# Delta rule in chunks: token products on 32-row tiles of the array, the state summed in PSUM

## The chip, the cores and the metric

The kernel runs on one core of a Trainium2 chip. The metric is the device time of one execution in microseconds (us), and lower is better. Five engines work side by side and meet at semaphores: PE (TensorE: "PE" rows are its matrix products, "PEld" rows the loads of its stationary operand), DVE (VectorE), ACT (ScalarE), POOL (GpSimd) and SP, which here only issues transfers (DMA). Each engine runs its own instructions in the order in which they were written down for it.

## The reference

Two blocks follow each other, all in fp32: a delta rule over 768 tokens (4 batch rows, 8 heads, head size 48), and a mixture of 8 experts with 4 slots each.

```python
k_n = k / (norm(k) + 1e-6)
for t in range(S):                       # S = 768; state: (B, H, 48, 48)
    y[:, :, t] = einsum('bhd,bhde->bhe', q[:, :, t], state)
    v_old = einsum('bhde,bhd->bhe', state, kt)
    state = state + bt * einsum('bhd,bhe->bhde', kt, vt - v_old)
x = y as (B*S, H*D) = (3072, 384)
logits = x @ phi                         # 32 slots
d = softmax of logits over the tokens;   slot_input = d.T @ x
slot_out[e] = relu(slot_input[e] @ w1[e]) @ w2[e]        # 8 experts, F = 1024
c = softmax of logits over the slots;    out = c @ slot_out
```

## The kernel before

The tokens are cut into 24 chunks of 32. Four chunks make a group, and there are six groups. On the 128 partitions lie four heads times 32 tokens (partition 32 h + t); the other head half g and the batch row b are looped over, so eight "units" u = (b, g) make up a chunk. In a chunk, with the state S before it:

    (I + L) w = V - Kn S,  L[t, s] = beta_s kn_t.kn_s (s < t),  u_s = beta_s w_s
    y = Q S + strict_lower(Q Kn^T) u,      S += Kn^T u

Names used below, with the lines of the kernel before. `psR` (L310) is Kn S, `R` (L314) is V minus it on DVE. `psW` (L324) is the inverse T applied to R, `U` (L329) is psW times beta on DVE. `psS` (L340) is Kn^T u, and `S` (L345) the state after it on DVE. `psY` gets Q S (L354) and then the strictly lower product with U (L359), and ACT copies it to `Y` (L362). A product over 32 tokens of each of four heads is made here with one stationary operand of 128x128 that is zero outside its four diagonal blocks: `TT` holds the inverse so, `AT` (L233) the lower product so, spread by DVE with the mask `bdm`, and `KX` (L291) the keys, spread by POOL with the mask `hm`. The chunk is worked in two halves `hf` of two batch rows each, so that DVE can work on one while PE works on the other.

What doesn't depend on the state runs one group ahead. `norm` scales the keys (`sq` L185, `ssq` L186, `Ks` L199). `prep` transposes keys and queries (L215, ACT copies them to `KQ`, L218) and makes the products over the head size (L230; ACT copies one half to `Lc`, L232, DVE makes `AT`). `invert` sends Lc through DRAM to the layout "one 32x32 block per partition" (`ld`, `lb`), multiplies by beta on POOL (L252), eliminates 31 columns on DVE (two instructions each, L264 and L267), and stores the inverse `tt` to DRAM (`td`). `near` loads a chunk's inverse from there into one of two `TT` buffers (L282). `route` makes logits (transposes L379, ACT copy `yT` L381, products with phi L385), both softmaxes, and the slots' weighted sums (`d` spread over heads L443, `db` on POOL L453, products L458) of the group before.

These steps are lists which `fill` interleaves with a chunk's chain: two `prep` in each of the chunks 0 and 1 of a group, `near`, half of `invert` and of `route` in chunk 2, the rest in chunk 3. A scheduler then sets each engine's final order. After the six groups come the routing of the last group, the experts (`ph` L557, `pso` L568) and the output (`pout` L588). Two experts' first weights `w1t` are loaded near the start; the others when the first block's memory is free. A matrix product in fp32 shows as two instructions in the profile, so 192 calls of L324 are 384 rows; transposes show as one.

Of the kernel before, what the change touches and what calls it, by code (L numbers as in the profile page):

```python
# [16 lines left out]
def kernel(  # L17
# [45 lines left out]
    wk = att.enter_context(tc.tile_pool(name="wk", bufs=2))  # L63

# [4 lines left out]
    Ks = [io.tile([P, GC, U, DP], F32, name=f"Ks{i}", bufs=1) for i in range(2)]  # L69
# [11 lines left out]
    def load_k(n, eng=nc.sync):  # L81
        load(k, Ks[n % 2], n, eng)
# [10 lines left out]
    NB = NCH // 3  # L93
    bts = []
    for i, tag in enumerate(("Lc", "lb", "tt")):
        t = wk.tile([U, NB, 4, C], F32, name=f"bt{i}", tag=tag, bufs=2 if tag == "tt" else 1)
        for h in range(4):
            nc.gpsimd.dma_start(
                out=t[:, :, h, :],
                in_=beta.rearrange("b (g h) (c t) -> h (b g) c t", h=4, t=C)[  # L100
                    h, :, i * NB:(i + 1) * NB])
        bts.append(t)
    # the same by blocks: partition 32 h + 8 c + u of a group of chunks
# [11 lines left out]
    for g in range(G):  # L115
# [12 lines left out]
                            pattern=[[C, 4]], channel_multiplier=-1)  # L128
    bdm = cpool.tile([P, 4, C], F32, name="bdm")
# [3 lines left out]
    nc.vector.tensor_tensor(bdm, bdm, hm.unsqueeze(2).broadcast_to([P, 4, C]), op=ALU.mult)  # L133
    sel = cpool.tile([P, GC, 4, C], F32, name="sel")
# [5 lines left out]
    bta = cpool.tile([P, NCH, U], F32, name="bta")  # L140
    pb = pt([P, NCH, U])
    for c in range(NCH):
        nc.tensor.transpose(pb[:, c, :], bts[c // NB][:, c % NB].rearrange("p h t -> p (h t)"),
                            ident[0:U, 0:U])
    nc.vector.tensor_copy(bta, pb)

    TTs = [wk.tile([P, U, 4, C], F32, name=f"TT{i}", bufs=1) for i in range(2)]
    for t in TTs:
        nc.vector.memset(t, 0.0)
    psS = ps.tile([P, 2, 4, D], F32, name="psS")  # L150
    nc.vector.memset(psS, 0.0)
    St = []
    for i in range(2):
        t = wk.tile([P, 2, 4, D], F32, name=f"S{i}", tag=f"S{i}")
        nc.vector.memset(t, 0.0)
        St.append(t)

# [16 lines left out]
    # Each of these gives a list of steps, which the chunks' chain is interleaved with.  # L174
    KQ, AT, KX, Lc, TTb = {}, {}, {}, {}, {}

    def norm(n):
        Kf = Ks[n % 2].rearrange("p c u d -> p (c u) d")
# [4 lines left out]
        def squares():  # L183
            sq = wk.tile([P, GC * U, D], F32, name="sq", tag="KX")
# [19 lines left out]
    def prep(n, c):  # L204
        """Of a chunk: Kn and Q transposed, strict_lower(Q Kn^T) and Kn Kn^T (both transposed)."""
        cc = n * GC + c

        def transposes(bh):
# [3 lines left out]
            for i in range(2):  # L212
                b = 2 * bh + i
                for a, src in enumerate((Ks[n % 2], Qs)):
                    nc.tensor.transpose(  # L215
                        tp[:, i, a, :],
                        src[:, c, b * G:(b + 1) * G, :].rearrange("p g d -> p (g d)"), ident)
            nc.scalar.activation(KQ[cc][:, 2 * bh:2 * bh + 2], tp, ACT.Copy)  # L218

        def products(g):  # L220
            if g == 0:
                AT[cc] = wk.tile([P, G, B, 4, C], F32, name="AT", tag="AT", bufs=2 * GC - 1)
                if c == 0:
                    Lc[n] = wk.tile([P, GC, B, G, C], F32, name="Lc", tag="Lc", bufs=1)
            r = slice(DP * g, DP * g + D)
            pg = pt([P, B, 2, C])
            for b in range(B):
                for h in range(4):
                    rh = slice(C * h, C * h + C)
                    nc.tensor.matmul(pg[rh, b], lhsT=KQ[cc][r, b, 0, rh], rhs=KQ[cc][r, b, :, rh],  # L230
                                     start=True, stop=True, skip_group_check=True)
            nc.scalar.activation(Lc[n][:, c, :, g, :], pg[:, :, 0, :], ACT.Copy)  # L232
            nc.vector.tensor_tensor(  # L233
# [389 lines left out]
```

## Time and profile before

| | |
|---|---|
| median of 3 runs | 919.21 us (918.97 to 921.51) |
| profiled execution, first to last instruction | 919.5 us |
| its mean granted TensorE clock | 0.701 |
| start, up to the first psW product | 97 us |
| group 0, up to the transposes in group 1 | 97 to 190 us |
| groups 1, 2 and 3 | 114.5, 114.8 and 115.4 us |
| group 4, up to the first psW product of group 5 | 127 us |
| group 5 | 48 us |
| routing of group 5, experts, output | 28, 151 and 31 us |

No time of the profiled execution outside its span is given; its span lies 0.3 us above the median, so the two are taken as the same. A timeline row reads: start in us, length in us, engine, line, operation, result and operands, shape, number of instructions, and in brackets how long the engine was idle before and what released it. A row of the stages reads: the stretch, its length, each engine's busy time (and instructions), the granted TensorE clock (1.00 is full speed), the share of DMA and its GB/s. A row of groups by line ends with "busy us, mean ns of one | idle before, releaser".

### The profile page before, as it was taken

The page shows a single profiled execution, that of the slowest core. Times are in us where ns is not written, and L with a number is a line of the kernel's source. Part 1 is how long each engine was busy: PE and PEld are TensorE (multiplying, and loading weights), DVE is VectorE, ACT ScalarE, POOL GpSimd, SP SyncE. Part 2 cuts the span into 40 slices and gives each one's busy share as a digit, 9 for nine tenths or more (in the row PEclk, how much of TensorE's full clock was granted, in tenths as well). Part 3 has the DMA queues.
Part 4 walks back from the last instruction along what each step waited for, and adds up shares of the span by engine and source line. Part 5 has one row for each costly group of instructions (what it writes and reads, how often), then busy time and mean ns, then how long its engine had stood idle before and what let it go on. Part 6 is the DMA issues. An engine that isn't in the chain of part 4 may idle for free.

```text
span 919.5 us, 19108 instructions
## 1 busy us (share of the span) xinstructions
PE 679.9 (74%) x8324; PEld 565.6 (62%) x8324; DVE 299.4 (33%) x816; ACT 101.3 (11%) x223; POOL 192.9 (21%) x347
## 2 busy tenths in 40 slices
PE   1706569069990799807998069996499799999998
PEld 1504569058880688706888058885398696765754
DVE  3267112942139421394213942226421100000011
ACT  0303000021120211102111021111000110000001
POOL 7231213131251213412134111351210200000000
PEclk9999999999995555755557555565555567667765
DMA  6240763023310242102321021000100099990013
GB/s 118 37 85 26 133 115 72 1 52 55 75 20 0 58 70 55 20 0 58 69 55 19 0 58 32 25 2 0 35 13 1 1 266 211 237 231 16 1 60 146
DMA packets 148019, 58.12 MB, mean 63 GB/s; under 512 B 131968, under 2 KB 143328, under 8 KB 147936
## 3 DMA queue, kind: packets, MB, share of 16 engines
q1 hardware_dynamic: 141888, 55.87, 27.9%
q10 hardware_dynamic: 5664, 0.94, 0.6%
q8 instruction: 65, 1.06, 0.5%
q0 software_dynamic: 384, 0.10, 0.1%
q14 instruction: 18, 0.15, 0.1%
HBM read 45.86 MB, written 11.01 MB: 62 GB/s over the span
## 4 chain that ended last, share of the span: by engine, by line
PE 64%; DVE 17%; DMA 6%; POOL 4%; SPq 3%; ACT 3%; issue 2%; ACTq 0%; DVEq 0%; POOLq 0%
PE ph L557 9%; PE psW L324 8%; PE psY L359 7%; DVE pr L264 7%; PE pso L568 6%; PE psS L340 6%; DVE tt L267 6%; PE pt L215 5%; PE pt L385 5%; PE pt L458 3%; PE pout L588 3%; PE psR L310 2%; PE pt L230 2%; PE psY L354 2%; PE pt L379 2%; SPq L77 2%
## 5 line engine op out<-in xcount | busy, mean ns | idle before, releaser
L215 PE MATMUL pt<-ident,Ks 128*128 128x128 f32 x96 | 42.1, 438 | 167.9 <-POOL Ks L199 158.7
L291 POOL TENSOR_TENSOR KX<-Ks,hm 128x192 f32<-128x192 f32 x184 | 91.0, 531 | 354.0 <-PE psS L340 264.4
L215 PEld LDWEIGHTS pt<-ident,Ks 128*128 128x128 f32 x96 | 20.8, 216 | 173.9 <-POOL Ks L199 159.6
L324 PE MATMUL psW<-R,TT 128*128 128x48 f32 x384 | 86.6, 396 | 34.4 <-DMA TT<-td 31.2
L324 PEld LDWEIGHTS psW<-R,TT 128*128 128x128 f32 x384 | 81.1, 311 | 39.4 <-DMA TT<-td 19.1
L557 PEld LDWEIGHTS ph<-sacc,w1t 96*128 96x128 f32 x512 | 87.8, 272 | 3.8 <-issue 3.8
L557 PE MATMUL ph<-sacc,w1t 96*128 96x4 f32 x512 | 88.1, 310 | 0.0
L359 PE MATMUL psY<-U,AT 128*128 128x48 f32 x384 | 83.9, 393 | 0.0
L264 DVE TENSOR_TENSOR pr<-tt,lb 128x31 f32<-128x31 f32 (+15 forms) x186 | 76.7, 413 | 16.2 <-POOL lb L252 11.0
L359 PEld LDWEIGHTS psY<-U,AT 128*128 128x128 f32 x384 | 78.2, 306 | 3.4
L267 DVE TENSOR_TENSOR tt<-tt,pr 128x31 f32<-128x31 f32 (+15 forms) x186 | 73.3, 394 | 5.2
L340 PE MATMUL psS<-U,KX 128*48 128x48 f32 x1472 | 69.8, 271 | 0.0
L340 PEld LDWEIGHTS psS<-U,KX 128*48 128x48 f32 x1472 | 60.8, 181 | 6.3 <-issue 1.7
L568 PE MATMUL pso<-w2t,hx 128*32 128x384 f32 x128 | 58.5, 627 | 1.7 <-DVE hx L561 1.7
L329 DVE TENSOR_TENSOR U<-psW,bta 128x192 f32<-128x192 f32 x48 | 17.2, 358 | 113.4 <-PE psW L324 113.4
L345 DVE TENSOR_TENSOR S<-S,psS 112x384 f32<-112x384 f32 x46 | 25.5, 554 | 87.6 <-PE psS L340 87.3
L233 DVE TENSOR_TENSOR AT<-pt,bdm 128x512 f32<-128x512 f32 x48 | 31.9, 688 | 62.1 <-ACT Lc L232 59.0
L385 PE MATMUL pt<-phi,yT 96*128 96x32 f32 x192 | 45.1, 398 | 6.0 <-ACT yT L381 5.1
L230 PE MATMUL pt<-KQ 48*32 48x64 f32 x1536 | 47.5, 310 | 1.9
L385 PEld LDWEIGHTS pt<-phi,yT 96*128 96x128 f32 x192 | 42.0, 323 | 10.5 <-ACT yT L381 9.1
L561 DVE TENSOR_SCALAR hx<-ph 128x32 f32<-128x32 f32 x8 | 1.5, 192 | 141.0 <-PE ph L557 141.0
L354 PE MATMUL psY<-S,KQ 48*32 48x48 f32 x1536 | 46.1, 265 | 0.1
(107 smaller groups left out, 698.9 us busy)
## 6 DMA issues: line engine op xcount, KB each, us to landing
w1t<-in_moe_w_dram SPq DMA_DIRECT2D x16, 768.0 KB
w2t<-in_moe_w_dram SPq DMA_DIRECT2D x8, 1536.0 KB
Ks<-in_k_dram SPq DMA_DIRECT2D x96, 48.0 KB
V<-in_v_dram SPq DMA_DIRECT2D x96, 48.0 KB
out_dram<-ob SPq DMA_DIRECT2D x24, 192.0 KB
Qs<-in_q_dram SPq DMA_DIRECT2D x80, 48.0 KB
ld<-Lc SPq DMA_DIRECT2D x24, 128.0 KB
lb<-ld SPq DMA_DIRECT2D x6, 512.0 KB
```

Source lines behind the costliest of these rows:

```text
L215: nc.tensor.transpose(tp[:, i, a, :], src[:, c, b * G:(b + 1) * G, :].rearrange("p g d -> p (g d)"), ident)
L230: nc.tensor.matmul(pg[rh, b], lhsT=KQ[cc][r, b, 0, rh], rhs=KQ[cc][r, b, :, rh], start=True, stop=True, skip_group_check=True)
L264: nc.vector.tensor_tensor(prv, tt[:, 0:m, j:j + 1].broadcast_to([P, m, w]), lb[:, j, j + 1:C].unsqueeze(1).broadcast_to([P, m, w]), op=ALU ...
L267: nc.vector.tensor_tensor(tt[:, 0:m, j + 1:C], tt[:, 0:m, j + 1:C], prv, op=ALU.subtract)
L291: nc.gpsimd.tensor_tensor(KX[cc][:, g, b], kn[:, b].unsqueeze(1).broadcast_to([P, 4, D]), hm.unsqueeze(2).broadcast_to([P, 4, D]), op=ALU. ...
L324: nc.tensor.matmul(pw[:, i, g, :], lhsT=T[:, (2 * hf + i) * G + g].rearrange("p h t -> p (h t)"), rhs=Rs[hf][:, i, g, :], start=True, stop ...
L340: nc.tensor.matmul(psS[DP * g:DP * g + D, i, h, :], lhsT=kx[:, g, 2 * hf + i, h, :], rhs=Us[hf][:, i, g, :], start=True, stop=True, skip_g ...
L354: nc.tensor.matmul(py[C * h:C * h + C, b, :], lhsT=kq[r, b, 1, C * h:C * h + C], rhs=old[b // 2][r, b % 2, h, :], start=(b == 0), stop=Fal ...
L359: nc.tensor.matmul(py[:, b, :], lhsT=at[:, g, b].rearrange("p h t -> p (h t)"), rhs=Us[b // 2][:, b % 2, g, :], start=False, stop=True, sk ...
L385: nc.tensor.matmul(pl, lhsT=yT[:, h].rearrange("p c t -> p (c t)"), rhs=phi[:, h, :], start=(h == 0), stop=(h == 3))
L557: nc.tensor.matmul(st["ph"][:, t, :], lhsT=w1t[e][:, h, t * P:(t + 1) * P], rhs=sacc[:, h, sl], start=(h == 0), stop=(h == 3))
L568: nc.tensor.matmul(pso, lhsT=hx[:, e, t, :], rhs=w2t[e][:, t, :], start=(e == 0 and t == 0), stop=(e == E - 1 and t == NFC - 1))
```

## The change

Every product over 32 tokens now uses four tiles of 32 rows of the array, one for each head, instead of one stationary operand of 128x128 with zeros. For psW and the lower part of psY, head h uses rows 32h to 32h+31 and columns 32h to 32h+31, and all four write one PSUM bank on different partitions. For psS, head h uses rows 32h and on, 48 columns at 64 g, and each head writes its own bank. So `TT` and `AT` lose their zeros, `KX` is gone (the keys are read where they lie), and `tri`, the mask of one head, takes the place of `bdm`.

The state is no longer added on DVE: psS stays in four PSUM banks and sums over all chunks, and after each chunk ACT copies the half g = 0 and DVE the half g = 1 into one of two state buffers. That state holds, for each head, the two g blocks on its diagonal, so psR and Q S are each 16 calls with 128 rows and 96 columns moved, where they were 32 calls with 48 rows and 48 columns. The beta of U is multiplied into the inverse before its store, by one POOL instruction. The two halves of a chunk are merged: one R, one U, one Y copy in a chunk. psR and psW share one bank, psY has one bank, and there are three key buffers instead of two. The products of `prep` take g innermost, into two buffers at once. `fill` counts four calls in a chunk instead of five. The beta loads and transposes of the start (`bts`, `bta`) are gone.

```diff
-    TTs = [wk.tile([P, U, 4, C], F32, name=f"TT{i}", bufs=1) for i in range(2)]
-    psS = ps.tile([P, 2, 4, D], F32, name="psS")
+    TTs = [wk.tile([P, U, C], F32, name=f"TT{i}", bufs=1) for i in range(2)]
+    psS = psp.tile([P, 4, 512], F32, name="psS")
...
         def store():
+            nc.gpsimd.tensor_tensor(st["tt"], st["tt"],
+                                    bb[:, n].unsqueeze(1).broadcast_to([P, C, C]), op=ALU.mult)
...
+            pg = [pt([P, B, 2, C]) for _ in range(G)]
             for b in range(B):
                 for h in range(4):
+                    for g in range(G):
...
+            for g in range(G):
+                nc.scalar.activation(Lc[n][:, c, :, g, :], pg[g][:, :, 0, :], ACT.Copy)
+                nc.vector.tensor_tensor(AT[cc][:, g], pg[g][:, :, 1, :],
+                                        tri.unsqueeze(1).broadcast_to([P, B, C]), op=ALU.mult)
...
-        def keys(g):
...
+        for a, dst in enumerate((pr, py)):
+            for b in range(B):
+                for h in range(4):
+                    nc.tensor.matmul(dst[hs[h], b].rearrange("p g d -> p (g d)"),
+                                     lhsT=kq[:, b, a, hs[h]], rhs=old[:, h, b, :],
+                                     start=(b == 0), stop=False, skip_group_check=True)
+            if a == 0:
+                R = wk.tile([P, U, D], F32, name="R", tag="R", bufs=1)
+                nc.vector.tensor_tensor(R, Vt[n][:, c], pr.rearrange("p b g d -> p (b g) d"),
+                                        op=ALU.subtract)
+        fill()
+        pw = ps.tile([P, U, D], F32, name="psW", tag="psRW")
+        for u in range(U):
+            for h in range(4):
+                nc.tensor.matmul(pw[hs[h], u], lhsT=T[hs[h], u], rhs=R[hs[h], u],
+                                 start=(u == 0), stop=True, skip_group_check=True)
+        Ut = wk.tile([P, U, D], F32, name="U", tag="U", bufs=1)
+        nc.vector.tensor_copy(Ut, pw)
+        fill()
+        if cc < NCH - 1:
+            for b in range(B):
+                for g in range(G):
+                    for h in range(4):
+                        nc.tensor.matmul(psS[DP * g:DP * g + D, h, b * D:(b + 1) * D],
+                                         lhsT=K[hs[h], c, b * G + g, 0:D],
+                                         rhs=Ut[hs[h], b * G + g],
+                                         start=(cc == 0 and b == 0), stop=True,
+                                         skip_group_check=True)
+            for g in range(G):
...
+                if g:
+                    nc.vector.tensor_copy(dst, src)
+                else:
+                    nc.scalar.activation(dst, src, ACT.Copy)
+            fill()
+        for b in range(B):
+            for g in range(G):
+                for h in range(4):
+                    nc.tensor.matmul(py[hs[h], b, g], lhsT=at[hs[h], g, b], rhs=Ut[hs[h], b * G + g],
+                                     start=False, stop=True, skip_group_check=True)
```

Two places show how the order moves. The first is PE in group 0, from the inverse of chunk 0 on. Before:

```order
L324 MATMUL psW<-R,TT_212 128x48 x8
L340 MATMUL psS<-U,KX 48x48 x16
L359 MATMUL psY<-U,AT 128x48 x8
L340 MATMUL psS<-U,KX 48x48 x16
L310 MATMUL psR<-S,KQ 32x48 x16
L354 MATMUL psY<-S,KQ 32x48 x18
L310 MATMUL psR<-S,KQ 32x48 x16
L354 MATMUL psY<-S,KQ 32x48 x14
```

The same place in the changed kernel:

```order
L299 MATMUL psW<-R,TT_177 32x48 x32
L309 MATMUL psS<-U,Ks_78 48x48 x32
L326 MATMUL psY<-U,AT 32x48 x32
L288 MATMUL psR<-S_182,KQ 32x96 x16
L288 MATMUL psY<-S_182,KQ 32x96 x16
```

A chunk of 112 products in two halves becomes one of 128 smaller ones in a single pass; the lower product stands between psS and the next psR, and Q S between psR and the next psW.

The second place is POOL at the end of group 1, around its work for the inverse of group 2 and the keys of group 3. Before:

```order
L291 TENSOR_TENSOR KX<-Ks_75,hm 128x192 x8
L399 TENSOR_TENSOR Call<-el,mx 128x128
L453 TENSOR_TENSOR db<-dr,hm 128x128 x16
L252 TENSOR_TENSOR lb<-lb,bb 128x1024
L185 TENSOR_TENSOR sq<-Ks_76 128x1536
L291 TENSOR_TENSOR KX<-Ks_75,hm 128x192 x8
L199 TENSOR_TENSOR Ks_76<-Ks_76,rn 128x32x48
L256 MEMSET tt 128x1024
```

In the changed kernel:

```order
L366 TENSOR_TENSOR Call<-el,mx 128x128
L420 TENSOR_TENSOR db<-dr,hm 128x128 x16
L236 TENSOR_TENSOR lb<-lb,bb 128x1024
L169 TENSOR_TENSOR sq<-Ks_78 128x1536
L183 TENSOR_TENSOR Ks_78<-Ks_78,rn 128x32x48
L255 TENSOR_TENSOR tt<-tt,bb 128x1024
L240 MEMSET tt 128x1024
```

The keys' spreading is gone from POOL's queue, and the multiplication by beta stands between the scaling of the keys and the store of the inverse.

More of the change, by code (lines that the diff above doesn't have):

```diff
@@ L295, in near @@
[L295 removed]
+        return [inverse]
     def chunk(cc, Yn, fill):
         n, c = divmod(cc, GC)
[L300 to L304 removed]
+        kq, T, at, K = KQ.pop(cc), TTs[cc % 2], AT.pop(cc), Ks[n % 3]
+        old, new = St[cc % 2], St[1 - cc % 2]
@@ new lines, in chunk @@
+        hs = [slice(C * h, C * h + C) for h in range(4)]
+        pr = ps.tile([P, B, G, D], F32, name="psR", tag="psRW")
+        py = ps.tile([P, B, G, D], F32, name="psY", tag="psY")
+        for a, dst in enumerate((pr, py)):
[8 more added lines that the diff above has]
+                                        op=ALU.subtract)
@@ L349, in chunk @@
[L349 to L362 removed]
+                dst = new[r, :, :, g * D:(g + 1) * D]
@@ L545 @@
     nc.gpsimd.memset(hx, 0.0)
-    pso = ps.tile([NSL, Dm], F32, name="pso", tag="psW")
+    pso = ps.tile([NSL, Dm], F32, name="pso", tag="psRW")
     def first(e):
@@ L586 @@
             i = n * B + b
-            po = ps.tile([P, Dm], F32, name="pout", tag=("psR", "psY")[i % 2], bufs=2)
+            po = (ps, pp2)[i % 2].tile([P, Dm], F32, name="pout", tag=("pt", "po")[i % 2], bufs=2)
             nc.tensor.matmul(po, lhsT=cT[:, n, b, :], rhs=so, start=True, stop=True)
```

139 lines of the change are left out of this document (27 added, 112 removed).

## The prediction

> **What bounds the kernel now.** I read the page first (shares, chain), then the stages, then PE's timeline in one group, and last what PE waited for.
>
> ```profile
> span 919.5 us, 19108 instructions
> PE 679.9 (74%) x8324; PEld 565.6 (62%) x8324; DVE 299.4 (33%) x816; ACT 101.3 (11%) x223; POOL 192.9 (21%) x347
> PE 64%; DVE 17%; DMA 6%; POOL 4%; SPq 3%; ACT 3%; issue 2%; ACTq 0%; DVEq 0%; POOLq 0%
> ```
>
> ```profile
> 304.20:419.00 114.80, 81.89 (x1275) 72.57 (x1275) 48.90 (x133) 16.26 (x35) 30.32 (x54) 0.54 0.20 40
> 534.40:660.00 125.60, 103.29 (x1366) 90.35 (x1366) 44.81 (x151) 18.57 (x41) 30.83 (x67) 0.55 0.11 26
> 660.00:709.00 49.00, 47.05 (x703) 43.52 (x704) 8.64 (x26) 2.32 (x7) 3.76 (x8) 0.50 0.07 11
> 737.00:888.00 151.00, 149.13 (x664) 106.85 (x662) 1.73 (x10) 3.30 (x6) 1.37 (x1) 0.67 0.63 146
> ```
>
> The 74% is a mean over stages. Group 2 (304 to 419) has 82 us of PE in 115; group 5 has 47 in 49 with only the chunks' chain. The experts (151 us), and the 28 us of routing before and 31 us of output behind them, hold no changed product, so I leave their 210 us as they are.
>
> PE's timeline in group 2 shows two parts: PE without a pause to 389, then nothing for 29 us:
>
> ```profile
> 316.95 1.94 PE L324 MATMUL psW<-R,TT 128*128 128x48 f32 x8
> 318.82 1.52 PE L340 MATMUL psS<-U,KX 128*48 128x48 f32 x32
> 320.27 3.65 PE L359 MATMUL psY<-U,AT 128*128 128x48 f32 x16
> 323.85 1.52 PE L340 MATMUL psS<-U,KX 128*48 128x48 f32 x32
> 325.31 0.60 PE L310 MATMUL psR<-S,KQ 48*32 48x48 f32 x32
> 325.64 0.73 PE L230 MATMUL pt<-KQ 48*32 48x64 f32 x16
> 366.22 0.87 PE L354 MATMUL psY<-S,KQ 48*32 48x48 f32 x32
> 367.02 1.94 PE L359 MATMUL psY<-U,AT 128*128 128x48 f32 x8
> 375.69 5.96 PE L458 MATMUL pt<-db,Y 128*96 128x128 f32 x32 [0.76 <-POOL db L453]
> 381.48 0.99 PE L324 MATMUL psW<-R,TT 128*128 128x48 f32 x8
> 419.02 0.47 PE L215 MATMUL pt<-ident,Ks 128*128 128x128 f32 x1 [29.49 <-POOL Ks L199]
> ```
>
> ```profile
> 318.93 0.36 DVE L329 TENSOR_TENSOR U<-psW,bta 128x192 f32<-128x192 f32 x1 [2.74 <-PE psW L324]
> 320.39 0.56 DVE L345 TENSOR_TENSOR S<-S,psS 112x384 f32<-112x384 f32 x1 [1.11 <-PE psS L340]
> 389.24 1.29 DVE L264 TENSOR_TENSOR pr<-tt,lb 128x31 f32<-128x31 f32 x1
> ```
>
> In the pause DVE eliminates the inverse of the next group, from 389.24. It starts after the last R of the chain, because DVE keeps its order; so a shorter chain pulls it forward, and both parts stay in series.
>
> **The price of a product.** From start to start: a 128x128 block costs (323.85 - 320.27)/16 = 224 ns, a psS product (two column tiles) 1.45/32 = 45 ns, Q S (four column tiles in one row group) 0.80/32 = 25 ns, psR, which alternates the two row groups, 0.33/32 = 10 ns. So an instruction of 48 columns holds its tile for 80 to 100 ns, and the rate is that over the tiles at work. That row tiles overlap too is seen within the products of prep, 64 columns each, where the counts are instructions in flight in slices of 0.1 us, about 0.3 us long each:
>
> ```profile
> 306.10:306.20 0.10, 0.05 (x4) 0.50 1.27 492
> 306.20:306.30 0.10, 0.10 (x8) 0.50 1.05 410
> 306.90:307.00 0.10, 0.10 (x8) 0.50 0.42 164
> 307.00:307.10 0.10, 0.10 (x16) 0.50 0.72 153
> ```
>
> While only one row group's data is there, four start in 0.1 us; when both groups' are there, eight. That is 25 and 12.5 ns.
>
> **The change, step by step, in a chunk at the clock of these rows.**
> - psW: 16 x 224 to 234 = 3.7 us becomes 64 instructions on four diagonal tiles, 90/4 = 22 ns: 1.4. Saved 2.3.
> - Lower part of psY: 16 x 224 = 3.6 becomes 64 x 22 = 1.4. Saved 2.2.
> - psS: 64 x 45 = 2.9 becomes 64 x 11 (eight tiles) = 0.7. Saved 2.2.
> - psR and Q S: 64 x 10 + 64 x 25 = 2.2 becomes 2 x 32 x 40 (96 columns, twice the time, four tiles) = 2.6. Lost 0.4.
> - Products of prep: 64 x 25 becomes 64 x 12.5. Saved 0.8.
> Sum 7.1 us. No row shows four row tiles at once, so the ends for the diagonal tiles are 11 ns (as psS with all eight) and 90 ns (one at a time). I take 22, since a tile's own time is known and the four share no rows, columns or partitions.
>
> What replaces the halves: U becomes one DVE copy of 384 elements, behind which PE has nothing. The last group shows the wait of a bare chain:
>
> ```profile
> 661.28 1.91 PE L324 MATMUL psW<-R,TT 128*128 128x48 f32 x8 [12.43 <-DMA TT<-td]
> 663.65 1.94 PE L324 MATMUL psW<-R,TT 128*128 128x48 f32 x8 [0.45 <-DVE U L329]
> 700.05 1.94 PE L324 MATMUL psW<-R,TT 128*128 128x48 f32 x8
> 709.26 1.07 PE L379 MATMUL pt<-ident,Y 128*96 128x128 f32 x4
> ```
>
> It is 0.45 with 192 elements in 0.36 us; with 384 (0.56, as S) about 0.8. The state copy is 768 elements, on DVE and ACT side by side: two S adds bound it by 1.1 us, and the lower product's 1.4 us on PE covers it. Were that cover gone (tiles faster than 15 ns), PE would wait for it. R's subtraction (0.56) lies beside Q S (1.3), Y's copy beside psR. A bare chunk is then 1.4 + 0.8 + 0.7 + 1.4 + 1.3 + 1.3 = 6.9 us; before, three chunks took 700.05 - 661.28 = 38.8, 12.9 each.
>
> A switch between tile shapes happens four times in a chunk. Before, psW to psS (318.82 - 316.95 = 1.87 for 8) exceeds 8 x 224 ns by 0.08 us, and psS to psR (1.46 for 32) by nothing. I take 0, upper end 0.08 x 4 x 21 = 7 us. The Trainium skill, TensorEngine Tiling (Array Packing), Key Properties, says that changing the tiling mode drains the array; the trace shows no drain of that size here, and by those rows the sum would be 7 us longer at most.
>
> DVE and POOL:
>
> ```profile
> L233 DVE TENSOR_TENSOR AT<-pt,bdm 128x512 f32<-128x512 f32 x48 | 31.9, 688 | 62.1 <-ACT Lc L232 59.0
> L252 POOL TENSOR_TENSOR lb<-lb,bb 128x1024 f32<-128x1024 f32 x6 | 11.5, 1913 | 23.2 <-DMA Ks<-in_k_dram 23.2
> ```
>
> ```profile
> 392.48 0.30 DVE L264 TENSOR_TENSOR pr<-tt,lb 128x135 f32<-128x135 f32 x1
> 413.20 0.48 DVE L264 TENSOR_TENSOR pr<-tt,lb 128x135 f32<-128x135 f32 x1
> ```
>
> AT shrinks fourfold (688 to about 280 ns), and prep waits for it: 0.3 us of each prep. KX leaves POOL. An elimination step of 135 elements takes DVE 0.30 us alone and 0.48 beside KX (410.7 to 415.1 in group 2), so I estimate 0.8 us less in a group. The new multiplication before the store has lb's size, 1.9 us; td and TT are queued behind it. In groups 1 to 4 TT has the time of the preps; before the first chunk and in group 5 nothing covers it: 1.9 each.
>
> **The sum.**
> - Groups 1 to 3: three chunks at 7.1 = 21.3; the last runs at twice the rate (psW 0.99 for 8), 3.5. Given back: 0.3 more for U in each chunk, and about 3 us where logits and maximum now find less work to hide their ACT and DVE steps; 4 in all. Preps 1.2 and elimination 0.8 gained. 23 each, 69.
> - Group 4: 20 for its PE part, and 3.5 because lb no longer stands behind KX, less the 1.9: 21.6.
> - Group 5: 661.28 to 709.26 is 48.0; 3 x 6.9 + 1.4 + 0.8 + 1.4 = 24.3. 23.7.
> - Start and group 0:
>
> ```profile
> 101.74 19.34 DMA w1t<-in_moe_w_dram
> 121.92 1.91 PE L324 MATMUL psW<-R,TT 128*128 128x48 f32 x8 [12.19 <-DMA TT<-td]
> 145.10 3.76 POOL L291 TENSOR_TENSOR KX<-Ks,hm 128x192 f32<-128x192 f32 x8 [8.54 <-PE psS L340]
> 160.95 1.14 DVE L264 TENSOR_TENSOR pr<-tt,lb 128x31 f32<-128x31 f32 x1
> 189.76 0.47 PE L215 MATMUL pt<-ident,Ks 128*128 128x128 f32 x1 [28.24 <-POOL Ks L199]
> ```
>
> Chunk 0's gain is lost: chunk 1's TT waits behind the experts' weights until 121.9. Preps and AT bring the start forward by 3.8, the multiplication takes 1.9, so 120.0. Three chunks follow, 2 x 7.1, then 6.5 to the last R: 140.7; lb, no longer behind KX, is ready about 141.9. The elimination starts 19 us earlier and is 0.5 faster: 19.5.
>
> 69 + 21.6 + 23.7 + 19.5 = 134. 919.5 - 134 = 786 us. The span is 0.3 us above the median of 919.21, which changes nothing.
>
> **Rivals.**
> 1. PE's clock rises (736 us, 0.22). Busy is not what raises it here:
>
> ```profile
> 770.00:775.00 5.00, 5.00 (x17) 1.71 (x16) 0.00 (x0) 0.00 (x0) 0.00 (x0) 1.00 1.09 301
> 895.00:900.00 5.00, 5.00 (x9) 2.57 (x8) 1.11 (x2) 0.98 (x2) 0.00 (x0) 0.50 0.42 157
> ```
>
> The first is pso, 128 rows streamed: full clock. The second is pout, 32 rows: half clock. The changed chunk streams all 128 rows most of 6.9 us, where before 224 ns went into 48 columns. Against it: the U wait in each chunk, the transposes, and DVE's 29 us. At double rate a chunk is 4.7 (U 0.8, state copy 1.3, R's subtraction 0.8 exposed): 2.2 saved in 15 cold chunks (3 in group 0, 2 in each of groups 1 to 4, 4 in group 5), 33. Of a group's 30 us of other PE work (82 - 4 x 12.9) I estimate a third at the higher rate, 4 saved in four groups, 17. Together 50.
>
> 2. Row tiles do not overlap in one PSUM bank (954 us, slower, 0.10). In the rows above the two row groups wrote different banks; in the change psW's four row tiles write one. If they take turns, an instruction costs 90 ns: 5.4 instead of 1.4, twice in a chunk, 8 us in 21 exposed chunks (3 in group 0, three and a warm half in groups 1 to 4, 4 in group 5), 168. It decides at 134/21/128 = 50 ns over my 22, so at 72 ns. TensorEngine Tiling, Restrictions and Gotchas, of the Trainium skill says just that row tiles cannot access the same bank at the same time; PSUM — Partial Sum Buffer there says different quadrants of one bank may be. No run here shows either yet.
>
> 3. Tiles half as parallel (849 us, 0.14): 45 ns, as psS with two. Then 64 x 23 ns more, twice in a chunk: 3.0 x 21 = 63. The change would do half of what it says.
>
> **How the numbers follow.** My forecast (786, own range 765 to 812) gets 0.52; 0.02 is left for gains that cancel. 725 to 850 holds the forecast, rival 3's center and most of rival 1: 8 in 10. Faster by over 0.3% (about what a measurement of this kernel can tell from no change) are the forecast and rivals 1 and 3, 0.88; within it the 0.02; slower is rival 2, 0.10.
>
> **What would show it.** psW and the lower psY near 1.4 us a chunk, psS 0.7, each in start-to-start time; chunks of 7 us in the last group; groups of 92 us with a pause near 28 us; psW of chunk 1 still waiting for TT at 120. I am wrong if diagonal tiles start one per 80 ns, if PE waits for ACT's or DVE's copies, or if the clock is over 0.7 inside the groups.

## The result, and the profile after

The changed kernel takes 778.0 us (776.01 to 786.86), the kernel before on the same chip 920.4. The ratio is 0.848, 95% interval 0.843 to 0.852. The profiled execution took 777.7 us, its span is 776.0. The prediction was 786 us, with an own range of 765 to 812. Times of the runs below are medians that leave out executions in a slower state (one of 1493.9 us of the kernel without tiles, one with the adds on DVE, two with the copies split by bank, one of the first changed order).

The page first: the span, the busy shares, and the shares of the chain that ended last.

```profile
span 776.0 us, 20231 instructions
PE 507.6 (65%) x9068; PEld 393.3 (51%) x9068; DVE 255.6 (33%) x694; ACT 112.6 (15%) x222; POOL 109.6 (14%) x158
PE 59%; DVE 19%; DMA 7%; ACT 4%; POOL 4%; issue 3%; SPq 2%; ACTq 0%
```

PE has 744 instructions more and is busy for 172 us less. The stages show where the time went (before and after from the two timelines, predicted from the sum):

| stage | before | predicted | after |
|---|---|---|---|
| start and group 0, up to group 1's transposes | 189.8 | 170.3 | 169.2 |
| groups 1, 2, 3 | 114.5, 114.8, 115.4 | 92 each | 92.3, 89.0, 90.3 |
| group 4 | 126.9 | 105.3 | 98.5 |
| group 5 | 48.0 | 24.3 | 27.5 |
| routing of group 5, experts, output | 210.2 | 210.2 | 209.2 |

PE in group 2, the timeline (start, length, line, operation, operands, shape, number):

```profile
263.38 1.87 PE L214 MATMUL pt<-KQ 48*32 48x64 f32 x64
265.97 0.47 PE L199 MATMUL pt<-ident,Ks 128*128 128x128 f32 x1 [0.72 <-DVE AT L219]
...
275.03 1.48 PE L299 MATMUL psW<-R,TT 32*32 32x48 f32 x58
276.44 0.45 PE L214 MATMUL pt<-KQ 48*32 48x64 f32 x12
277.16 1.07 PE L309 MATMUL psS<-U,Ks 32*48 32x48 f32 x64 [0.27 <-DVE U L302]
278.16 1.50 PE L326 MATMUL psY<-U,AT 32*32 32x48 f32 x64
...
283.36 0.86 PE L299 MATMUL psW<-R,TT 32*32 32x48 f32 x58
284.15 0.52 PE L214 MATMUL pt<-KQ 48*32 48x64 f32 x32
...
350.52 0.47 PE L199 MATMUL pt<-ident,Ks 128*128 128x128 f32 x1 [27.07 <-POOL Ks L183]
```

From start to start, psW is 1.41 us for 58 (24 ns each) at 275.03 and 0.79 for the same 58 at 283.36: the clock has doubled in between. The lower psY is 1.44 for 64 (22.5 ns), psS 1.00 for 64 (15.6 ns). The pause ahead of the next group is still there, 27.07 us.

The same group cut where the clock changes (stretch, length, busy time of PE, PEld, DVE, ACT and POOL, granted clock, share of DMA, GB/s), then two rows of the kernel before:

```profile
261.50:280.70 19.20, 17.28 (x413) 13.69 (x414) 3.20 (x9) 6.22 (x14) 3.47 (x3) 0.50 0.32 68
280.70:298.00 17.30, 14.44 (x527) 11.64 (x525) 4.06 (x9) 4.72 (x9) 0.00 (x0) 0.99 0.53 90
298.00:316.00 18.00, 16.30 (x206) 14.01 (x205) 5.40 (x22) 4.61 (x8) 5.89 (x17) 0.53 0.47 97
316.00:323.50 7.50, 5.44 (x263) 4.31 (x261) 2.61 (x6) 2.58 (x3) 4.95 (x4) 1.00 0.02 4
```

```profile
304.20:376.00 71.80, 68.84 (x1020) 60.16 (x1021) 17.30 (x54) 14.09 (x31) 13.56 (x30) 0.50 0.31 62
376.00:389.30 13.30, 12.81 (x252) 12.31 (x255) 3.68 (x13) 1.95 (x3) 8.44 (x16) 0.84 0.08 15
```

Before, the clock rose in the last 13 us of PE's part of this group only. After, it is at 0.99 for 17 us in the middle as well. The means of the two profiles, 0.701 before and 0.655 after, must not be read as a lower clock: the trace before has no record of the clock ahead of 264 us, and its rows read 1.00 there, although psW takes 1.94 us for 8 at 201.66 as it does at 0.50 in group 2.

A chunk without other work is seen in group 0, PE first, then the state's two copies:

```profile
115.86 2.00 PE L299 MATMUL psW<-R,TT 32*32 32x48 f32 x64 [15.63 <-DMA TT<-td]
118.52 1.07 PE L309 MATMUL psS<-U,Ks 32*48 32x48 f32 x64 [0.65 <-DVE U L302]
119.52 1.50 PE L326 MATMUL psY<-U,AT 32*32 32x48 f32 x64
121.48 1.63 PE L288 MATMUL psR<-S,KQ 128*32 128x96 f32 x32 [0.46 <-DVE S L319]
122.76 1.44 PE L288 MATMUL psY<-S,KQ 128*32 128x96 f32 x32
124.12 0.88 PE L299 MATMUL psW<-R,TT 32*32 32x48 f32 x64
```

```profile
119.62 0.80 ACT L321 ACTIVATE S<-psS 48x768 f32<-48x768 f32 x1 [22.15 <-PE psS L309]
120.46 0.96 DVE L319 COPY S<-psS 48x768 f32<-48x768 f32 x1 [2.00 <-ACT S L321]
```

It takes 8.3 us (115.86 to 124.12), and DVE's copy starts when ACT's has ended. About 0.5 us of it is the start of psW, whose first eight rows follow slowly on the wait for TT; the other 56 start 22 ns apart.

### The profile page after: what moved, and what is told of

It is laid out like the page before. It is cut to its first block, busy times and chain, and to the rows that moved or that the text cites. A ratio compares the mean times of both kernels' runs of the same rounds, so it can differ in the third digit from the quotient of the medians.

```text
span 776.0 us, 20231 instructions
## 1 busy us (share of the span) xinstructions
PE 507.6 (65%) x9068; PEld 393.3 (51%) x9068; DVE 255.6 (33%) x694; ACT 112.6 (15%) x222; POOL 109.6 (14%) x158
## 4 chain that ended last, share of the span: by engine, by line
PE 59%; DVE 19%; DMA 7%; ACT 4%; POOL 4%; issue 3%; SPq 2%; ACTq 0%
PE ph L524 11%; PE pso L535 7%; DVE tt L251 7%; DVE pr L248 7%; PE pt L199 5%; PE pt L352 5%; PE pt L425 4%; PE psW L299 4%; PE psR L288 4%; PE pout L556 4%; PE pt L214 3%; PE psY L326 3%; DMA TT<-td 2%; PE psS L309 2%; PE pt L346 2%
## 5 line engine op out<-in xcount | busy, mean ns | idle before, releaser
L199 PE MATMUL pt<-ident,Ks 128*128 128x128 f32 x96 | 39.9, 418 | 172.1 <-POOL Ks L183 137.7
L299 PE MATMUL psW<-R,TT 32*32 32x48 f32 x1536 | 37.2, 233 | 35.4 <-DMA TT<-td 32.9
L299 PEld LDWEIGHTS psW<-R,TT 32*32 32x32 f32 x1536 | 28.4, 127 | 45.7 <-issue 23.5
L425 PE MATMUL pt<-db,Y 128*96 128x128 f32 x192 | 35.4, 356 | 8.3 <-POOL db L420 8.3
L202 ACT ACTIVATE KQ<-pt 128x512 f32<-128x512 f32 x48 | 28.5, 597 | 76.9 <-PE pt L199 76.9
L288 PE MATMUL psR<-S,KQ 128*32 128x96 f32 x768 | 34.2, 313 | 7.7 <-DVE S L319 6.0
L302 DVE COPY U<-psW 128x384 f32<-128x384 f32 x24 | 13.4, 558 | 77.6 <-PE psW L299 77.6
L199 PE MATMUL pt<-ident,Qs 128*128 128x128 f32 x96 | 38.3, 403 | 0.0
L214 PEld LDWEIGHTS pt<-KQ 48*32 48x32 f32 x1536 | 28.4, 138 | 18.8 <-ACT KQ L202 10.1
L420 POOL TENSOR_TENSOR db<-dr,hm 128x128 f32<-128x128 f32 x96 | 35.7, 411 | 13.6 <-ACT dr L415 13.6
L425 PEld LDWEIGHTS pt<-db,Y 128*96 128x96 f32 x192 | 31.8, 223 | 11.5 <-POOL db L420 10.2
L321 ACT ACTIVATE S<-psS 48x768 f32<-48x768 f32 x23 | 18.5, 804 | 127.7 <-PE psS L309 127.7
```

Of the source, the lines that this page charges most:

```text
L199: nc.tensor.transpose(tp[:, i, a, :], src[:, c, b * G:(b + 1) * G, :].rearrange("p g d -> p (g d)"), ident)
L214: nc.tensor.matmul(pg[g][rh, b], lhsT=KQ[cc][r, b, 0, rh], rhs=KQ[cc][r, b, :, rh], start=True, stop=True, skip_group_check=True)
L288: nc.tensor.matmul(dst[hs[h], b].rearrange("p g d -> p (g d)"), lhsT=kq[:, b, a, hs[h]], rhs=old[:, h, b, :], start=(b == 0), stop=False, ...
L299: nc.tensor.matmul(pw[hs[h], u], lhsT=T[hs[h], u], rhs=R[hs[h], u], start=(u == 0), stop=True, skip_group_check=True)
L420: nc.gpsimd.tensor_tensor(db[:, b], st["dr"][:, c, b].unsqueeze(1).broadcast_to([P, 4, NSL]), hm.unsqueeze(2).broadcast_to([P, 4, NSL]), o ...
L425: nc.tensor.matmul(pa.rearrange("p h s -> p (h s)"), lhsT=Yn[:, c, b, :], rhs=db[:, b].rearrange("p h s -> p (h s)"), start=(b == 0), stop ...
```

## The experiments

### One part at a time

Two kernels separate the tiles from the rest. One takes psW and the lower psY of the changed kernel back to 128x128:

```diff
-                nc.tensor.matmul(pw[hs[h], u], lhsT=T[hs[h], u], rhs=R[hs[h], u], ...)
+            nc.tensor.matmul(pw[:, u], lhsT=T[:, u].rearrange("p h t -> p (h t)"), rhs=R[:, u], ...)
-                    nc.tensor.matmul(py[hs[h], b, g], lhsT=at[hs[h], g, b], ...)
+                nc.tensor.matmul(py[:, b, g], lhsT=at[:, g, b].rearrange("p h t -> p (h t)"), ...)
```

> The changed kernel with only psW and the lower part of psY back on block-diagonal weights of 128x128 (TT and AT with zeros again, AT spread with bdm; everything else as changed: merged halves, psS on row tiles, state summed in PSUM, beta in the inverse; AT has 6 buffers and tt one, to make room). Theory (the gain is the array time that four tiles at once save): psW and the lower product go from 1.45 us back to 3.6 us each in a chunk at the low clock, 4.3 us in 21 exposed chunks = 90 us; AT costs DVE 0.4 us more in a product, some 5 us in all; and where the clock had risen inside the groups it falls back, up to 15 us: 865 to 890 us. Rival (the gain comes from merging the halves, from the state sum in PSUM and from shorter DVE and POOL queues): under 820 us. In the profile psW should take 3.6 us for 16 instructions and the granted clock between 262 and 300 us should be near 0.50 instead of 0.5 to 1.0.

The other gives the kernel before the tiles alone:

```diff
-                    nc.tensor.matmul(pw[:, i, g, :], lhsT=T[:, (2 * hf + i) * G + g]..., rhs=Rs[hf][:, i, g, :], ...)
+                        nc.tensor.matmul(pw[rh, i, g, :], lhsT=T[rh, (2 * hf + i) * G + g, h, :], rhs=Rs[hf][rh, i, g, :], ...)
-                nc.tensor.matmul(py[:, b, :], lhsT=at[:, g, b].rearrange("p h t -> p (h t)"), ...)
+                    nc.tensor.matmul(py[rh, b, :], lhsT=at[rh, g, b, h, :], ...)
```

> The kernel before with one part of the change alone: psW and the lower psY on four diagonal tiles (the 32x32 blocks of TT and AT as they lie, zeros unread), halves, KX, state add and all else as before. Theory: 3.6 + 3.6 us become 1.45 + 1.45 in a chunk; 4.3 us in 21 exposed chunks = 90 us, so 830 us, down to 805 if the clock rises inside the groups as well. Rival (the merged halves, the PSUM sum and the freed POOL carry the gain): over 870 us.

Measured: with the tiles alone 815.3 us (ratio 0.886, 0.882 to 0.890), so they bring 104 us. Without them 828.3 us (0.902, 0.897 to 0.906), so they are worth 50 there, and the rest alone brings 91. The first is inside its range, the second fits neither its theory nor its rival: 104 + 91 is 195, and both together bring 141. Something is gained by either part and only once. A further profile of the kernel without tiles was taken to look for it.

> The kernel of e1_blocks once more, for a profile. It took 828 us, 50 more than the changed kernel, where 90 were expected, and the tiles alone had brought the kernel before 104 us. Theory: the clock makes up the difference. The products of the state that now stream all 128 rows raise the granted clock inside the groups here too, so some of the block-diagonal products run at twice the rate: group 2 shows 0.60 or more (before 0.54), and psW takes 3.6 us in a cold chunk and 1.9 in a warm one. Rival: the clock stays near 0.54 and the block products are covered by other work: then PE waits less for U, S and the routing than in the changed kernel.

It took 832.2 us in its one execution. psW of the four chunks in group 2, then two stretches of that group, then two of group 1 in the kernel with the tiles alone:

```profile
293.82 3.65 PE L301 MATMUL psW<-R,TT 128*128 128x48 f32 x16
...
307.43 2.23 PE L301 MATMUL psW<-R,TT 128*128 128x48 f32 x16
...
315.89 1.99 PE L301 MATMUL psW<-R,TT 128*128 128x48 f32 x16
...
340.60 1.88 PE L301 MATMUL psW<-R,TT 128*128 128x48 f32 x16
```

```profile
281.50:307.00 25.50, 23.00 (x381) 19.99 (x382) 6.12 (x11) 6.15 (x14) 3.46 (x4) 0.50 0.35 71
307.00:324.00 17.00, 15.97 (x350) 14.39 (x349) 4.40 (x9) 5.12 (x10) 0.00 (x0) 0.97 0.50 98
```

```profile
180.30:200.00 19.70, 18.34 (x438) 14.59 (x442) 6.57 (x17) 5.64 (x13) 2.27 (x5) 0.54 0.36 76
200.00:232.00 32.00, 30.68 (x891) 25.32 (x888) 10.82 (x35) 8.22 (x17) 13.27 (x30) 0.85 0.51 96
```

The clock fits that something, as the theory of that profile had it. It rises 18 us into the group with the tiles alone, 27 us into it without them and 19 in the changed kernel, and in the kernel before only at the end. A block-diagonal psW costs 3.6 us in the cold chunk (at the low clock) and about 2 in the three others, so going back to it, and to the lower product, costs 2 x 2.2 us once and 2 x 1.1 three times. That is an estimate of 11 us in a group and 55 in five, where 50 was measured and 90 expected. No run holds the clock fixed, so how much of the 54 us between 195 and 141 it explains is not shown. Nor were the parts of the rest (psS on row tiles, the merged halves, KX gone from POOL) run one by one.

### Do the tiles overlap, and what decides it?

The changed kernel with the loop over heads outside, so that neighbours in PE's queue use one tile (cut; the lower psY is changed in the same way):

```diff
-        for u in range(U):
-            for h in range(4):
+        for h in range(4):
+            for u in range(U):
                 nc.tensor.matmul(pw[hs[h], u], ...
```

> The changed kernel with psW and the lower psY in another order alone: all eight units of one head, then the next head, so that neighbours in PE's queue use the same tile of the array. Theory (a tile is held 80 to 100 ns by an instruction, and only different tiles overlap): 64 instructions take 64 x 90 = 5.8 us instead of 1.45 at the low clock, half of that at the high one; 4.3 us twice in 21 exposed chunks, of which a third at the high clock: 120 to 180 us more, 900 to 960 us. Rival A (an instruction costs 22 ns whatever tile it uses, the rate is that of PE's issue): 778 us, no change. Rival B (the tiles overlap by halves only): 840 us.

Measured: 898.0 us (0.977, 0.974 to 0.981), 120 more than the changed kernel with the same instructions, 2 us under the theory's range and far from both rivals. psW's and psY's rows at the low clock:

```profile
304.02 1.48 PE L299 MATMUL psW<-R,TT 32*32 32x48 f32 x16
305.44 0.47 PE L199 MATMUL pt<-ident,Qs 128*128 128x128 f32 x1
...
313.82 4.40 PE L326 MATMUL psY<-U,AT 32*32 32x48 f32 x64
318.16 0.45 PE L214 MATMUL pt<-KQ 48*32 48x64 f32 x12
```

An instruction holds its tile 89 ns in psW (1.42 / 16) and 68 in psY (4.34 / 64; why less, no row tells). With the tiles in turn it is 22 to 24. So four row tiles do run at once, into one PSUM bank on different partitions, and the order of issue decides whether they do.

### The state sum

```diff
-                                         start=(cc == 0 and b == 0), stop=True,
+                                         start=(b == 0), stop=True,
-                if g:
-                    nc.vector.tensor_copy(dst, src)
-                else:
-                    nc.scalar.activation(dst, src, ACT.Copy)
+                nc.vector.tensor_tensor(dst, old[r, :, :, g * D:(g + 1) * D], src, op=ALU.add)
```

> The changed kernel with only the state sum undone: psS holds one chunk's product, and DVE adds it to the old state into the new one, both halves g, instead of the sum in PSUM with a copy by ACT and one by DVE. Theory: the copies already run one after the other (in the trace DVE's starts when ACT's has ended, 0.80 then 0.96 us), so two adds of 768 elements on DVE, about 1.0 us each, take 0.2 to 0.3 us longer in a chunk: 4 to 7 us, 782 to 785 us; summing in PSUM by itself buys nearly nothing. Rival (the sum in PSUM is a main part of the gain, since the state leaves DVE): over 800 us.

Measured: 780.1 us (0.847, 0.843 to 0.850), the same as the changed kernel and 2 us under the theory's range. Two adds on DVE take as long as the two copies in series (1.94 us against 0.80 + 0.96 and the step between them). Summing in PSUM by itself buys nothing here.

```profile
277.67 1.94 DVE L318 TENSOR_TENSOR S<-S,psS 48x768 f32<-48x768 f32 x2 [0.51 <-PE psS L309]
```

### The copies of the state

Split by bank, at first inside one psS tile:

```diff
-            for g in range(G):
-                ...
+            for hh in (slice(0, 2), slice(2, 4)):
+                for g in range(G):
+                    dst = new[r, hh, :, g * D:(g + 1) * D]
+                    src = psS[r, hh, 0:B * D].rearrange("p h (b d) -> p h b d", d=D)
+                    # DVE for heads 2 and 3, ACT for 0 and 1
```

> The changed kernel with the state's copy split by PSUM bank alone: ACT copies heads 0 and 1, DVE heads 2 and 3 (two instructions each, for g = 0 and 1), instead of ACT g = 0 and DVE g = 1 of all four banks. Theory (the two copies run one after the other, 0.80 then 0.96 us, because both touch the same four banks, so the state is late for psR by 0.46 us in a cold chunk and 1.08 in a warm one): they run side by side, the state is ready about 1.1 us after psS instead of 1.8, and the 6.0 us that PE waits for S go: 770 to 774 us. Rival (they wait for one another, or for PE, for another reason): 778 to 784 us with the wait as it is.

Measured: 780.2 us (0.847, 0.843 to 0.850), in the rival's range, though PE's wait for S fell from 6.0 to 3.1 us. DVE still starts after ACT; its instruction waits for ACT's semaphore in the program. So sharing the banks is not the reason. With psS as two tiles:

> The changed kernel with psS as two tiles of two banks each (heads 0 and 1, heads 2 and 3); ACT copies the first, DVE the second, two instructions each. With one tile and the same split the copies still ran one after the other, since DVE's instruction waits for ACT's semaphore in the program. Theory (that wait is the whole reason): DVE's copy starts with ACT's, the state is ready 1.1 us after psS, the 6.0 us that PE waits for S are gone, 770 to 774 us. Rival (the chip itself runs two readers of psS in turns): the two copies take 0.9 us and more each where they overlap, and the time stays at 778 us.

Measured: 780.2 us (0.847, 0.845 to 0.850). The first pair of rows is the one tile, the second the two, and the last a row of the waits of the kernel with two (total, times, longest):

```profile
95.86 0.99 ACT L322 ACTIVATE S<-psS 48x384 f32<-48x384 f32 x2 [8.84 <-PE psS L309]
...
96.89 1.12 DVE L320 COPY S<-psS 48x384 f32<-48x384 f32 x2 [2.19 <-ACT S L322]
```

```profile
94.36 0.99 ACT L322 ACTIVATE S<-psS 48x384 f32<-48x384 f32 x2 [8.80 <-PE psS L309]
94.42 1.12 DVE L320 COPY S<-psS 48x384 f32<-48x384 f32 x2 [1.20 <-PE psS L309]
```

```profile
PE psR L288 <- issue: 7.8, 8, 1.6
```

The copies now run side by side and take 0.99 and 1.12 us as they did in series, so the common tile was the reason. The wait for DVE's S is gone, and 2.1 us for ACT's are left. But the time is not shorter: psR now has 7.8 us of "issue", where PE waits for nothing that the profile shows (1.6 in the changed kernel). The theory was right on the order of the copies and wrong on the time. What stands behind "issue" is told in the last section.

### The clock by itself

```diff
+        if c == 0 and 1 <= n <= 4:
+            for _ in range(40):
+                pk = pt([P, U * D])
+                nc.tensor.matmul(pk, lhsT=ident, rhs=R.rearrange("p u d -> p (u d)"), start=True, stop=True)
```

> The changed kernel with PE kept busy in the pause ahead of groups 2 to 5 (the DVE elimination): 40 products of 128x128 weights with 384 columns, result unread, behind the last R and ahead of the next transposes. It computes the same. Theory (the clock follows what PE streams in the last microseconds): it stays at 1.00 through the pause, a product takes about 0.65 us, 26 in all, and the 20 us of preps and of chunk 0 behind it run at up to twice the rate: 7 to 9 us in each of four groups, 745 to 755 us; so a good part of a group is a matter of the clock. Rival A (the clock falls whatever PE does, by time or by a budget): the 40 products take 52 us, 25 more than the pause: 860 to 880 us. Rival B (the clock is up but the preps wait for ACT and DVE): 770 to 778 us.

Measured: 766.0 us (0.833, 0.830 to 0.835): 12 us, half or less of the 23 to 33 expected, and between the theory's range and that of rival B. The stretches ahead of group 3 and into it:

```profile
314.60:339.00 24.40, 24.33 (x76) 14.04 (x74) 22.89 (x59) 0.23 (x1) 2.70 (x1) 1.00 0.00 1
339.00:347.00 8.00, 5.12 (x147) 3.77 (x147) 1.35 (x6) 3.06 (x8) 3.57 (x4) 1.00 0.31 87
347.00:358.00 11.00, 10.56 (x307) 8.62 (x311) 2.01 (x4) 3.53 (x7) 0.00 (x0) 0.53 0.40 67
```

While 128 rows stream the clock stays at 1.00 (rival A is out). The preps behind them run at the high clock for 8 us, and then it falls in the midst of them, PE being 96% busy. So a busy PE holds the clock up in one kind of work and not in the other, and in the 8 us at the high clock PE is busy for 5.1 only, since the preps then wait for ACT and DVE, as in rival B.

### Orders that the profile suggested

The first moves the slots' sums behind elimination steps on DVE (and the product with beta, `lb`, ahead of `db` on POOL); in short:

```diff
+    behind(first db of a group, marks["lb"]);  behind(each slots' sum, marks["el"])   # order of issue only
```

> The changed kernel with another order of DVE and POOL in groups 1 to 4 alone: beta's multiplication into lb stands ahead of the routing's spread of d on POOL, and the sums of the slots stand behind 8 (then 2 more each) elimination steps on DVE, so that the slots' products move from ahead of the last chunk into the elimination. Theory (the chain of chunks and the elimination lie in series, and all that is taken out of the chain from the last Y to the last R shortens the group): the slots' 5.8 us and the 1.2 us wait for db leave the chain, 6 to 7 us in four groups: 750 to 755 us. Rival (the chunks lose what the slots gave: the cold clock comes back without them, or U and S queue behind the elimination on DVE): 775 us or more.

Measured: 753.7 us (0.818, 0.815 to 0.821), as the theory said. The second concerns the pause itself.

```diff
-                if c == 1:
-                    load_q(n + 2)
-                elif c == 2:
-                    load_k(n + 2)
-                elif c == 3:
-                    drain(norm(n + 2))
+                if c == 0:
+                    load_k(n + 2)
+                elif c == 1:
+                    load_q(n + 2)
+                    drain(norm(n + 2))
```

> The changed kernel with the keys of the group after next loaded one chunk into a group and normed after chunk 1 (the third key buffer is free then), instead of after chunks 2 and 3; nothing else. Theory: the pause of 27 us ahead of groups 2 to 5 is not the elimination's length as such. PE waits there for the normed keys, and their norm stands in DVE's queue behind 25 of the 31 elimination steps. With the norm ahead, the transposes and products of a group (20 us of PE) run inside the pause, and what is left to wait for is TT: the elimination's end and 9 us of store and loads behind it. psW of chunk 0 comes 4 us earlier, and the 6 us of preparation that now lie behind it are gone: 8 to 10 us in each of four groups, 738 to 746 us. Rival: POOL's squares and scaling (2.8 us each) now fall into the chain of chunks and hold DVE up there, as a step of 31 elements beside them took 2.63 instead of 0.18 us: 5 us given back in each group, 760 to 778 us.

Measured: 738.7 us (0.801, 0.798 to 0.804), inside the theory's range. The last product of the preps, now inside the pause, and the psW that ends it:

```profile
238.19 1.26 PE L214 MATMUL pt<-KQ 48*32 48x64 f32 x64 [0.25 <-ACT KQ L202]
263.58 0.75 PE L299 MATMUL psW<-R,TT 32*32 32x48 f32 x4 [24.13 <-DMA TT<-td]
```

Together, with the experts' weights moved:

> The edits of e5_early, e12_norm and e7b_two_tiles together, and the experts' first two weights loaded in the pauses ahead of groups 1 and 2 instead of ahead of chunk 1's TT. It computes the same. Theory (the four shorten different stretches): slots out of the chain 23 us, norm 32 to 40, state copies 6, and in group 0 the TT of chunk 1 no longer behind the weights (15.6 us of wait, some 5 of which the preparation of group 1's inverse takes back): 700 to 715 us. Rival (they all empty the same pause, and the elimination with its store and loads is then the bound): 725 us or more.

Measured: 728.0 us (0.792, 0.789 to 0.795), in the rival's range: the parts do not add up. The rival's reason is part of it at most: PE still waits 55.9 us for TT, but two stalls of 6.6 us for nothing shown came on top. Its waits led to the last kernel, whose edits the expectation names.

> The kernel of e13_all with three edits: on POOL the normed keys stand ahead of the routing's Call, so that the norm's sum on DVE no longer waits ahead of U; the experts' first weights are loaded in four halves of 768 KB in four pauses instead of twice 1.5 MB; the first slots' sum stands behind 10 elimination steps instead of 8. It computes the same. Theory: U's 3.1 to 3.8 us of wait in three groups go, and the two stalls of 6.6 us, in which PE had nothing to issue while the weights filled all 16 DMA engines, become about 3 us each inside pauses that have room: 712 to 718 us. Rival (the elimination with its store and loads bounds a group, and PE's waits only move): 725 us or more; a stall of 6 us with half the weights would say that it isn't the transfer that starves PE.

Measured: 720.1 us (0.783, 0.777 to 0.789), the fastest of all, some 2 us over the range. U's wait of 3.8 us is still there once. The two stalls of 6.6 us became three of 3.9, 4.8 and 3.6, one with each of three halves of the weights, so that 12.3 us of 13.2 stayed; the rival's sign, a stall of 6 us with half the weights, did not come.

## Why the prediction came out, point by point

**The price of a product: right for the diagonal tiles.** 22 ns was taken from ends of 11 and 90; psW has 24 and psY 22.5. Rivals 2 and 3 (72 and 45 ns) are out. The rule weighed there, of the Trainium skill's TensorEngine Tiling (Array Packing), Restrictions and Gotchas, that row tiles cannot access one bank at the same time, does not hold for psW, whose four tiles share a bank on different partitions; the wording of the Trainium skill's PSUM — Partial Sum Buffer, Terms, that different quadrants of a bank may be accessed at once, agrees with the 24 ns. Row tiles that write the same partitions of a bank were not tried here.

**Terms of the chunk that were mis-sized.** psS takes 15.6 ns, not 11, so it saved 1.9 us, not 2.2. The products of prep did not gain 0.8 us in a chunk but nothing: 64 take 1.87 us (263.38), and before the same 64 took 1.90.

```profile
306.15 1.90 PE L230 MATMUL pt<-KQ 48*32 48x64 f32 x64
308.68 0.47 PE L215 MATMUL pt<-ident,Ks 128*128 128x128 f32 x1 [0.63 <-DVE AT L233]
```

That step read two slices of 0.1 us and took a burst for the rate. The 1.2 us of a group from a smaller AT did not come either: DVE's AT fell from 688 to 284 ns, but PE's wait named after it is 0.72 us (265.97) for 0.63 before (308.68), since the AT itself waits for ACT's Lc. "Side by side" for the state's copies was wrong: they run in series, 1.8 us instead of 1.1, and psR waits 0.46 us in a cold chunk and up to 1.08 in a warm one. U's wait (0.8 taken, 0.65 to 0.76 measured) and psR and Q S (1.3 each, 1.28) were right. The bare cold chunk is 8.3 us, not 6.9: psW up to psS 2.66 for 2.2 (its slow start), psS 1.00 for 0.7, psY up to psR 1.96 for 1.4, Q S up to psW 1.36 for 1.3.

**Rival 1 came true in part, and hid that.** "The clock over 0.7 inside the groups" was named as what would make me wrong. It was 0.99 for 17 of the 62 us of PE's part of group 2. There PE was busy 14.4 us, so at half the clock the stretch would have been up to 14 us longer, an estimate, and the group up to 103 us instead of 89 where the sum said 92. So at a constant clock the sum may have been up to 11 us too good in a group; the clock gave about as much, and the two errors cancelled. The separate parts fit this: each raises the clock alone (0.85 and 0.97 in the rows above). That the total came within 8 us is therefore luck in part: the tiles' price was right, the rest of the sum half so. Two slips inside the rivals change no verdict: four times 4 us are 16 and not 17, and 64 products at 90 ns are 5.8 us and not 5.4.

**Stages.** Group 4 gained 28.4 us for 21.6 predicted. In its order more of the routing stands between chunks, and its clock was 0.67 for 0.55 before; I take that as the cause, but no run tests it alone. Group 5 gained 20.5 for 23.7: its first psW starts slowly over 1.2 us as TT arrives (539.29 to 540.44), its next three chunks, cold to warm, take 8.7, 7.7 and 6.1 us, and in each a transpose of the routing, queued ahead of psR, waits 0.61 us for ACT's Y, which the sum did not have. In the start, psW of chunk 1 came at 115.9 for 120.0. That was not the work of the preps, as the prediction had it: group 1's preps there took 14.9 us from first to last start, 13.4 before. But POOL scales the keys at 64.48 instead of 69.91, since KX (5.43 us there) no longer stands ahead, and the experts' weights, with TT behind them, start earlier too. The elimination of group 1 was bound by lb as predicted, so the group began at 169.2 for 170.3.

**The pause: right size, wrong cause.** "DVE keeps its order; so both parts stay in series" predicted a pause near 28 us, and it is 27. But PE waits in it for the normed keys, not for the inverse (137.7 us in all, in five pauses):

```profile
PE pt L199 <- POOL Ks L183: 137.7, 5, 29.9
```

Their norm only stands late in DVE's queue. With it ahead, the preps fit into the pause and 39 us go (738.7). The row that said so was in the prediction, "29.49 <-POOL Ks", and was read as if it named the elimination.

## What to carry to other kernels

Put products that contract over 32 rows on row tiles, and issue them so that neighbours use different tiles: the same 64 instructions took 1.4 us in turns, and in a row 4.3 (psY) or, by psW's 89 ns, 5.7. Price such a change once at each clock, since two parts may both be paid by the same rise of the clock. And read what a pause waits for word by word: the releaser named in its row may be ordinary work that only stands late in another engine's queue.

## What the runs showed of the hardware that was not expected

**A busy PE was not enough to raise its clock.** Before, PE was busy 68.8 of 71.8 us in group 2 at 0.50; after, from 124.2 to 142.0 us in group 0, it was busy 10.7 of 17.8 us at 0.78. The Trainium skill, TensorE: Matmul & The Clock Gate, What's actually happening, says that some 3.4 us of sustained work lead to the full clock; if busy time in the profile is what it means by work, the 0.50 contradicts it for this mix of small fp32 products, and the 24 us of 128-row streams at 1.00 fit it. Tiles at work and rows streamed both grew here; which counts is open.

**A long POOL instruction stopped DVE for its whole length.** In group 2's pause DVE's last product of 31 elements takes 2.63 us beside POOL's scaling of the keys; the first one, at 323.31 and alone, takes 0.18. In the pause ahead of group 1 a step of 192 elements takes 2.78 us (145.65) beside POOL's squares, and 0.36 alone (327.97):

```profile
347.66 2.81 POOL L183 TENSOR_TENSOR Ks<-Ks,rn 128x1536 f32<-128x1536 f32 x1 [26.71 <-DVE pr L248]
...
347.88 2.63 DVE L248 TENSOR_TENSOR pr<-tt,lb 128x31 f32<-128x31 f32 x1
```

This agrees with the Trainium skill, SBUF — State Buffer, SBUF: two separate sides: a DVE operation with two SBUF inputs and a GpSimd operation take turns at a shared port, each for a whole instruction.

**PE waits for its instructions.** In the kernel of the joint edits PE stood for 6.65 us, waiting for nothing that the profile shows, while 1.5 MB of weights filled the 16 DMA engines (first row), and with half the weights for 3.92, 4.81 and 3.61 us (two of them below):

```profile
133.00:139.80 6.80, 0.18 (x2) 0.05 (x1) 0.00 (x0) 0.60 (x1) 1.91 (x1) 0.69 1.01 168
```

```profile
139.83 0.37 PE L207 MATMUL pt<-ident,Ks 128*128 128x128 f32 x1 [6.65 <-issue]
```

```profile
213.04 0.70 PE L297 MATMUL psY<-S,KQ 128*32 128x96 f32 x21 [3.92 <-issue]
294.36 1.19 PE L297 MATMUL psY<-S,KQ 128*32 128x96 f32 x23 [4.81 <-issue]
```

The trace has a DMA queue for instructions. In the changed kernel it moves 71 packets of 16 KB, and PE has 18,136 products and weight loads, 255 for each packet (before: 65 packets, 16,648 and 256). All four stalls end 1.3 to 1.5 us after such a packet has landed: at 138.38 us, for one, with PE going on at 139.83. So do the short stalls of 0.2 to 2.2 us in the changed kernel, 13 in all with 11 us: each ends 1.2 to 1.6 us after a packet, and so do the 19 of 0.2 us or more up to 600 us in the kernel with two psS tiles. Where the products take longer, in the kernel before and with tile after tile, PE has no such stall. So PE waits there, by all that the traces show, for its next packet, which comes late most of all when other transfers fill the engines. A chunk of the changed kernel is 512 such instructions, two packets. That this is why the two psS tiles did not shorten the time is likely, but no run tests it by itself.
